# Moving taps and transposes off VectorE, pairing its exponential chains, and doubling convolution streams in an attention-and-convolution kernel

## The chip, the cores and the metric

The kernel runs on one core of one Trainium2 chip. A core has TensorE (PE), VectorE (DVE), ScalarE (ACT), GpSimd (POOL) and SyncE (SP), the last used here to issue transfers. The metric is device time in microseconds (us), the median of the runs of one program. Bytes are moved by 16 DMA engines.

## What is computed

Two independent halves are computed and concatenated along the last axis. S = 2048 positions, D = 640 channels, bf16.

```python
# half A: a gated long convolution
k_shift[s] = sum_t k[s - t] * shift_k[:, t]        # 4 taps, per channel
kv = k_shift * v
y  = causal_convolution(kv, ssm_k)                 # per channel, length 2048 (by FFT in the reference)
a  = q * (y + kv * ssm_D)
# half B: attention with H = 32 heads of 20 channels
q, k, v = split(x @ wqkv)
p = softmax(q @ k.T / sqrt(20));  b = (p @ v) @ wo
out = concatenate([a, b], -1)                      # (1, 2048, 1280)
```

## The kernel before

**Attention.** The scores are computed transposed, in blocks of 128 keys x 512 queries. There are 4 query chunks, 8 groups of 4 heads and 16 key blocks, so 512 steps of 4 heads: 2048 such blocks, numbered as units (`NU`). A unit is one matmul with 20 rows of the array (`S_task`, L594); up to three units go into neighbouring PSUM banks, in two alternating halves of three banks. One ScalarE instruction takes the exponential of two or three banks at once and writes bf16 into slots of `P_sb` (`EXP_task`, L635, L640). `NPU` = 24 slots exist. `PV_task` (L681) multiplies four slots with V, which carries a column of ones for the softmax sum, and frees them. At the end of a group VectorE copies the sums out (L700), TensorE transposes them and VectorE divides (L706 to L721); the output projection follows (L766).

**Exponentials on VectorE.** Part of the units goes to VectorE instead, in a chain of seven instructions per unit (`chain_start`, L651): L664 reads PSUM, scales and adds so that the uint16 result is nearly the bit pattern of the bf16 exponential; L666 takes the low seven bits; L667, L668, L670 and L671 form a polynomial correction; L672 adds it. All but L664 read and write SBUF only. `want_vec` (L1134) decides, for each third bank, whether it goes to VectorE: only if the planned queue of VectorE is below `VQ` = 3 us, and not for the last two key blocks of a group.

**The order of work is written by a planner.** The Python code keeps an estimated clock per engine (`Prog.op`, L141) with a cost for every instruction, and while it emits the program it picks what TensorE and VectorE do next by what would be ready and by due times. Projections (`KQ_task`, L490; `V_task`, L498), transposes of x (`XT_task`, L434) and output tasks are put in a list with due times, counted in steps of four units (L1046 and the lines after). Matmuls on zeros (`zeros`, L346, L349) are put in when the planned TensorE stream of the last 3.4 us is under `ZTH` = 1.8 us. What the hardware executes is this fixed order per engine, with semaphore waits.

**Half A, taps.** x and k arrive with positions on partitions. For x, TensorE transposes 128x128 tiles into PSUM (L420) and VectorE or ScalarE copies them to `xT` (L432, L430). For k, `kv_iter` (L528) gets four shifted copies of k from memory per tile of 128 positions and does the four taps and the product with v on VectorE: eight operations of 128x640 per tile (L531), 16 tiles. The product goes to scratch in memory, once in order (`kv_scratch`) and once with reversed blocks of 32 (`kvr_scratch`).

**Half A, convolution.** When the taps are done, `conv_setup` (L866) starts it. A channel's convolution is a product with a Toeplitz matrix, whose tiles are read from the padded kernels in memory with a step of one element between partitions: `hk_load` (L887) loads 4 x [32, 2112] per quarter task, into one of four buffers. Per quarter task 32 matmuls run (L929), with 128 rows of weights each and 16 x shrinking numbers of columns, 5120 in all. The moving operand is built by 80 GpSimd copies (`kvx_build`, L893, L899) into a buffer whose other channels are zero. VectorE adds the halves out of PSUM (L947, L948, L950). `A_iter` (L963, L969) then does the product with D, the sum and the product with q on VectorE, three operations of 128x320 for each of 32 pieces.

Of the kernel before, what the change touches and what calls it, by code (L numbers as in the profile page):

```python
# [6 lines left out]
ALU = mybir.AluOpType  # L7
FP32 = mybir.dt.float32
BF16 = mybir.dt.bfloat16
I32, I16, U16 = mybir.dt.int32, mybir.dt.int16, mybir.dt.uint16  # L10

S = 2048
# [11 lines left out]
HKW = 2112  # L24
NHK = 4
NPU = 24
NQS = 10
NU = NB * 4
NPAIR = 48
NXB = 3  # L30
KV0, KVPACE, APACE, VQ, CONVE, ZTH, AGE, WAIT3 = 30.0, 0.75, 0.5, 3.0, 60, 1.8, 14, 0.3
TAND = 0.287
# [3 lines left out]
EXP_C = (0.07826797, 0.30457564)  # L36
LAT = {"pe": 0.12, "act": 0.1, "dve": 0.06, "pool": 0.1}
# [42 lines left out]
class Prog:  # L80
    ENGS = ("sp", "act", "pe", "dve", "pool")

    def __init__(self, nc, enter):
# [11 lines left out]
        self.stream = []  # L95
        self.sem = {e: self.newsem("s_" + e) for e in self.ENGS if e != "sp"}
# [44 lines left out]
    def op(self, eng, fn, reads=(), writes=(), tok=True, dsem=None, extra=(), n=1, c=0.1, kb=0.0, st=0.0, kind="f", two=False, me=None):  # L141
# [42 lines left out]
        if dsem is not None:  # L184
            self.dma_t = max(self.dma_t, start + 1.7) + kb / 215
            when = self.dma_t + 0.5
# [33 lines left out]
    def dmas(self, eng, pairs, dsem, reads=(), writes=()):  # L220
# [3 lines left out]
        def fn(e):  # L224
            for i, (out, in_) in enumerate(pairs):
                ins = e.dma_start(out, in_)
                if i + 1 < len(pairs):
                    ins.then_inc(s, 16)
            return ins
        kb = 0.0  # L230
        for out, _ in pairs:
# [3 lines left out]
            kb += e  # L235
        return self.op(eng, fn, reads, writes, dsem=dsem, n=len(pairs), c=0.43 * len(pairs), kb=kb)
# [10 lines left out]
def build_kernel(nc, A_q, A_k, A_v, A_shift_k, A_ssm_k, A_ssm_D, B_x, B_wqkv, B_wo, out):  # L247
# [3 lines left out]
    with ExitStack() as es:  # L251
# [15 lines left out]
        P_sb = sb("P_sb", [128, NPU, 512])  # L267
# [4 lines left out]
        XV_sb = sb("XV", [128, NXB, 512], U16)  # L272
        XF_sb = sb("XF", [128, NXB, 3, 512])
# [3 lines left out]
        Dbc = sb("Dbc", [128, D])  # L277
        ident = sb("ident", [128, 128])
        ZS = sb("ZS", [128, 256], FP32)
        rden = sb("rden", [128, 32], FP32)  # L280

        HK_E, KVR_E, KVX_E, Y_E, AST_E = HKW, 64 * 80, 8 * 256, 16 * 320, 320
        ph0 = NCC * 2 * D + 4 * 4 * D + 2 * 5 * D + KS * D + 2 * D + 2 * D
        ph1 = NHK * HK_E + KVR_E + 2 * KVX_E + 2 * Y_E + 5 * AST_E
        xT = sb("xT", [128, NCC, S])
        WQ = sb("WQ", [128, NCC, D])
        R = sb("R", [128, max(ph0, ph1)])
# [8 lines left out]
        xst = [carve(4 * D).rearrange("p (t d) -> p t d", t=4) for _ in range(4)]  # L296
        kst = [carve(5 * D).rearrange("p (j d) -> p j d", j=5) for _ in range(2)]
        Ctile = carve(KS * D).rearrange("p (j d) -> p j d", j=KS)
        tA, tB = carve(D), carve(D)
        kvst = [carve(D) for _ in range(2)]  # L300
        pos[0] = 0
        HK = [carve(HK_E) for _ in range(NHK)]
        KVr = carve(KVR_E).rearrange("p (j c) -> p j c", j=64)
        KVX = [carve(KVX_E) for _ in range(2)]
        Y = [carve(Y_E).rearrange("p (t c) -> p t c", t=16) for _ in range(2)]
        Aq = [carve(AST_E) for _ in range(3)]
        Akv = [carve(AST_E) for _ in range(2)]
# [8 lines left out]
        kvd = nc.dram_tensor("kv_scratch", (S, D), BF16).ap()  # L316
        kvr_d = nc.dram_tensor("kvr_scratch", (S, D), BF16).ap()

        b_ident, b_ones, b_tA, b_tB, b_C, b_ZS = (Buf() for _ in range(6))
        b_WK0, b_WQ0, b_Wa, b_Wb, b_Wo, b_D = (Buf() for _ in range(6))  # L320
        b_xst = [Buf() for _ in range(4)]
# [3 lines left out]
        b_XV, b_XF, b_XQ, b_XP = ([Buf() for _ in range(NXB)] for _ in range(4))  # L325
# [8 lines left out]
        b_kst = [Buf(), Buf()]  # L334
        b_kvst = [Buf(), Buf()]
        b_kvd, b_kext, b_kshT = [], Buf(), Buf()
# [27 lines left out]
        def x_load(n):  # L364
            return P.dma("sp", xst[n], ap(x2, [[D, 128], [128 * D, 4], [1, D]], n * 512 * D), DS("x%d" % n),
                         writes=[b_xst[n]])

        b_x0 = [Buf() for _ in range(4)]
        for i in range(4):
            P.dma("sp", xst[0][:, i, :], x2[i * 128:(i + 1) * 128, :], DS("x0%d" % i), writes=[b_x0[i]])  # L370
# [1011 lines left out]
```

## Time and profile before

The median of three runs is 880.22 us (878.06 to 895.95). The profiled execution has a span of 882.1 us and took 883.89 us.

| what | from the profile of before |
|---|---|
| span | 882.1 us |
| units on ScalarE / on VectorE | 1845 / 203 |
| matmuls of the convolution (L929) | 5120 |
| GpSimd copies (L899) | 80, 1368 ns each |
| matmuls on zeros (L349) | 178 |
| loads of convolution weights | 640, 132 KB each |
| mean DMA rate | 146 GB/s |

In the profile a group line has the form "line, engine, operation, written tile <- read tile, shape, count | busy us, mean ns of one | idle time before it, and the releaser of most of it". The rows of digits cut the span into 40 slices of 22 us; a digit is the busy share in tenths, in the row PEclk the TensorE clock that was granted. A table by stage has, after the stage and its length, the busy us of each engine with the number of instructions in brackets, then the granted clock, the share of DMA time and GB/s. Neighbouring instructions of an engine overlap a little, so the sum of groups is larger than the engine's busy time.

### The profile page before, as it was taken

To read this page: it belongs to the slowest core of one execution; us is meant where nothing else is said; L and a number is where in the kernel's file an instruction comes from. 1 tells how busy PE (TensorE), PEld (TensorE's weight loads), DVE (VectorE), ACT (ScalarE), POOL (GpSimd) and SP (SyncE) were. 2 spreads that over 40 slices of the span, in tenths; PEclk is the share of its full clock that TensorE was granted. 3 is DMA by queue.
4 is the path that set the end of the run, shared out by engine and by line. 5 is a ranking of instruction groups with operands and counts; after the bars stand their busy time and mean duration, and the time that the engine had idled before them with its cause. 6 is when DMAs were issued, how large, how long until landed. Compare 5 with 4: busy or idle time off the path is not lost.

```text
span 882.1 us, 26786 instructions
## 1 busy us (share of the span) xinstructions
PE 831.9 (94%) x11389; PEld 389.3 (44%) x11402; DVE 770.3 (87%) x1993; ACT 843.9 (96%) x731; POOL 121.0 (14%) x94
## 2 busy tenths in 40 slices
PE   9999999988999999999999999899999999989887
PEld 5432332222345545545545545444454554545422
DVE  4469999999479998999899999999899999989963
ACT  6699999999779999999999999999999999999996
POOL 3000000001402220122210220220120122010000
PEclk9999999999569999999999999999999999999999
DMA  9614333334736556565669656767454465645243
GB/s 298 208 58 153 105 106 106 106 106 75 149 90 174 162 155 174 165 163 149 184 172 172 169 150 180 192 174 193 133 148 127 136 178 139 174 125 159 56 109 86
DMA packets 83603, 129.19 MB, mean 146 GB/s; under 512 B 34561, under 2 KB 60283, under 8 KB 83483
## 3 DMA queue, kind: packets, MB, share of 16 engines
q1 hardware_dynamic: 81323, 124.36, 52.5%
q0 software_dynamic: 704, 2.74, 0.8%
q8 instruction: 90, 1.47, 0.7%
q10 hardware_dynamic: 1456, 0.37, 0.2%
q14 instruction: 30, 0.25, 0.1%
HBM read 116.81 MB, written 13.23 MB: 147 GB/s over the span
## 4 chain that ended last, share of the span: by engine, by line
DVE 48%; PE 27%; ACT 22%; issue 2%; DMA 1%; DVEq 0%; SPq 0%
ACT P_sb L640 22%; DVE XV L664 9%; PE PS L929 8%; PE PS L598 8%; DVE XF L671 6%; DVE P_sb L672 6%; DVE XF L670 5%; PE PS L690 5%; DVE R L531 3%; DVE XF L667 3%; DVE XF L666 3%; DVE XF L668 3%; PE PS L446 2%; PE PS L349 2%; DVE R L950 2%
## 5 line engine op out<-in xcount | busy, mean ns | idle before, releaser
L640 ACT ACTIVATE P_sb<-PS 128x1536 bf16<-128x1536 f32 (+1 forms) x723 | 839.4, 1356 | 24.6 <-PE PS L598 23.6
L598 PE MATMUL PS<-QT,KT 20*128 20x512 bf16 x2048 | 286.3, 392 | 25.6 <-ACT P_sb L640 17.1
L929 PE MATMUL PS<-R 128*128 128x128 bf16 (+15 forms) x5120 | 250.3, 195 | 2.4 <-DVE Bout L764 1.0
L929 PEld LDWEIGHTS PS<-R 128*128 128x128 bf16 x5120 | 200.8, 98 | 113.2 <-issue 112.8
L690 PE MATMUL PS<-P_sb,V_sb 128*21 128x512 bf16 x2048 | 179.1, 391 | 9.5 <-DVE P_sb L672 8.4
L899 POOL COPY R<-R 32x512 bf16<-32x512 bf16 x80 | 109.4, 1368 | 449.4 <-PE PS L929 438.6
L664 DVE TENSOR_SCALAR XV<-PS 128x512 uint16<-128x512 f32 x203 | 139.2, 686 | 32.2 <-PE PS L598 31.4
L598 PEld LDWEIGHTS PS<-QT,KT 20*128 20x128 bf16 x2048 | 70.4, 91 | 181.3 <-ACT P_sb L640 130.5
L672 DVE TENSOR_TENSOR P_sb<-XF,XV 128x512 uint16<-128x512 bf16 x203 | 90.3, 445 | 4.8
L671 DVE TENSOR_TENSOR XF<-XF 128x512 bf16<-128x512 bf16 x203 | 90.2, 444 | 3.6
L670 DVE TENSOR_TENSOR XF<-XF 128x512 bf16<-128x512 bf16 x203 | 87.7, 432 | 0.0
L690 PEld LDWEIGHTS PS<-P_sb,V_sb 128*21 128x21 bf16 x2048 | 38.6, 89 | 91.0 <-issue 46.7
L667 DVE TENSOR_SCALAR XF<-XF 128x512 bf16<-128x512 uint16 x203 | 64.7, 319 | 1.9
L531 DVE TENSOR_TENSOR R<-R 128x640 bf16<-128x640 bf16 x128 | 61.6, 487 | 3.6 <-DMA R<-in_A_v_dram 0.7
L668 DVE TENSOR_SCALAR XF<-XF 128x512 bf16<-128x512 uint16 x203 | 63.0, 310 | 0.0
L349 PE MATMUL PS<-Zt 128*128 128x512 bf16 x178 | 58.3, 421 | 1.3 <-DVE Zt L343 1.0
L666 DVE TENSOR_SCALAR XF<-XV 128x512 uint16<-128x512 uint16 x203 | 57.2, 301 | 0.2
L446 PE MATMUL PS<-xT,WQ 128*20 128x512 bf16 (+1 forms) x660 | 46.4, 374 | 1.8 <-DVE R L950 0.8
L446 PE MATMUL PS<-xT,R 128*20 128x512 bf16 (+2 forms) x660 | 45.2, 374 | 0.4 <-DVE QT L432 0.2
L504 PE MATMUL PS<-R,xT 128*128 128x160 bf16 (+1 forms) x240 | 31.3, 257 | 1.0 <-ACT P_sb L640 0.8
L432 DVE CAST KT<-PS 128x512 bf16<-128x512 f32 (+1 forms) x32 | 21.6, 674 | 11.2 <-PE PS L446 11.1
L876 POOL MEMSET R<- 128x2048 bf16 x2 | 3.7, 1826 | 188.4 <-PE PS L690 188.4
(54 smaller groups left out, 339.7 us busy)
## 6 DMA issues: line engine op xcount, KB each, us to landing
R<-kext_scratch SPq DMA_DIRECT2D x640, 132.0 KB, 2.9
R<-in_A_k_dram SPq DMA_DIRECT2D x15, 640.0 KB, 3.9
kext_scratch<-in_A_ssm_k_dram POOLq DMA_DIRECT2D x1, 2560.0 KB, 14.3
R<-in_A_v_dram SPq DMA_DIRECT2D x16, 160.0 KB, 5.4
kv_scratch<-R SPq DMA_DIRECT2D x16, 160.0 KB
kvr_scratch<-R SPq DMA_DIRECT2D x16, 160.0 KB
R<-kvr_scratch SPq DMA_DIRECT2D x8, 320.0 KB, 7.0
R<-in_A_q_dram SPq DMA_DIRECT2D x32, 80.0 KB, 2.1
```

The lines of the kernel that those rows point to most:

```text
L446: ins = e.matmul(bank[bk][32 * i:32 * i + DH, 0:n], Wt[:, cc, off + i * DH:off + (i + 1) * DH], xT[:, cc, x0:x0 + n], start=(cc == 0), sto ...
L598: ins = e.matmul(bank[b0 + i], KT[32 * u:32 * u + DH, g, kb * 128:(kb + 1) * 128], QT[32 * u:32 * u + DH, qs(qc, g), :], start=True, stop= ...
L640: P.op("act", lambda e: e.activation(P_sb[:, s0:s0 + m, :], PS[:, b0 * 512:(b0 + m) * 512].rearrange("p (u q) -> p u q", u=m), ACT.Exp, sc ...
L664: (lambda e: e.tensor_scalar(V, bank[bk], scale * 1.4426950408889634 * 128.0, 127.0 * 128.0, op0=ALU.mult, op1=ALU.add), [bkb[bk]], [bv], ...
L667: (lambda e: e.tensor_scalar(Q, F.bitcast(U16), -128.0, None, op0=ALU.add), [bf], [bq], 0.287, True),
L668: (lambda e: e.tensor_scalar(C, F.bitcast(U16), a / 16384.0, b / 128.0, op0=ALU.mult, op1=ALU.add), [bf], [bc], 0.287, True),
L670: (lambda e: e.tensor_tensor(Q, Q, F.bitcast(U16), ALU.mult), [bf, bq], [bq], 0.421, True),
L671: (lambda e: e.tensor_tensor(Q, Q, C, ALU.mult), [bq, bc], [bq], 0.421, True),
L672: (lambda e: e.tensor_tensor(P_sb[:, z, :].bitcast(U16), Q, V, ALU.add), [bv, bq], [b_P[z]], 0.421, True)], end)
L690: ins = e.matmul(bank[OBANK][32 * u:32 * u + DH + 1, :], V_sb[:, kb, 4 * g + u, :], P_sb[:, slot[4 * b + u], :], start=first, stop=last, t ...
L899: P.op("pool", lambda e, dst=dst, src=src: e.tensor_copy(dst, src), reads=[cv["KVr"]], writes=[cv["KVX"][i]] if X == 3 else [], extra=(cv[ ...
L929: P.op("pe", lambda e, o=o, lhsT=lhsT, rhs=rhs, st=st, last=last: e.matmul(o, lhsT, rhs, start=st, stop=last, skip_group_check=True), read ...
```

## The change

Five things change together, with a retuned planner.

- x and k are loaded by transposing transfers directly into the layout with channels on partitions. The transposes on TensorE and their evacuations go away.
- The four taps become matmuls on TensorE: the transposed k, shifted by one column per tap, against diagonal matrices `Dg` that GpSimd builds once (20 tasks of 16 matmuls, `C_task`). VectorE multiplies the sum in PSUM by v while it takes it out. The D term is folded into the first element of each convolution kernel, so that `kv_scratch` and two of the three final operations disappear; the third, the product with q, goes to GpSimd in 128 pieces of 128x160.
- Two exponential chains on VectorE run as one: each unit has its own PSUM read, and the other operations take both units, 128x1024, six instructions for two. `want_vec` is allowed a planned queue of 5 us and opens no pair in the last three key blocks of a group.
- The convolution is retiled: 16 channels per task, weights as 4 x [32, 4, 544] per quarter task; each matmul streams its operand and, beside it, an equal number of zeros into other columns, 52 to 64 columns in all.
- GpSimd's copies and products are each put beside a VectorE instruction that reads PSUM (`pool_beside`). Loads and stores on SyncE are issued in the order in which the planner expects them to be ready.

P slots grow from 24 to 36, four of which become free only when the taps' buffers are dead. The filler goal is 2.1 us in 3.4.

The core of the diff:

```diff
-NPU = 24
+NPU, NPX = 36, 4
+OBS = 20
-KV0, KVPACE, APACE, VQ, CONVE, ZTH, AGE, WAIT3 = 30.0, 0.75, 0.5, 3.0, 60, 1.8, 14, 0.3
+KBV, KBW, LONE = 13, 12, 16
+CQ = 0.026
+KV0, KVS, VQ, CONVE, ZTH, AGE, WAIT3 = 52, 2.5, 5, 80, 2.1, 40, 0.2
...
+        if turn:
+            def fn(e):
+                return e.dma_start_transpose(*pairs[0])
...
+        def x_load(t, n):
+            return P.dmas("sp", [(xT[:, :, t * 128:(t + n) * 128], x2[t * 128:(t + n) * 128, :])], DS("x%d" % t),
+                          writes=b_xT[t:t + n], slow=1.3, turn=True)
...
-        def kv_iter():
...
+        def C_task(c, h, bk):
...
+                    for j in range(KS):
+                        ins = e.matmul(bank[bk][:, n * 128:(n + 1) * 128], kT[i][:, cc, 16 + 128 * t - j:144 + 128 * t - j],
+                                       Dg[:, j, cc, :], start=(n + j == 0), stop=(j == KS - 1), skip_group_check=True)
...
+            work(1, [(lambda e: e.tensor_tensor(o, p, v, ALU.mult), [bkb[bk], b_vst[i]], [b_kvst[i]], 0.69, False)], after)
...
+            V, F, Q = XV_sb[:, i, 0:512 * m], XF_sb[:, f, 0, 0:512 * m], XF_sb[:, f, 1, 0:512 * m]
+            one, two = 0.154 + 0.1335 * m, 0.154 + 0.267 * m
...
+                (lambda e: e.tensor_scalar(F.bitcast(U16), V, 127, None, op0=ALU.bitwise_and), bv, [bf], one, True),
+                (lambda e: e.tensor_scalar(Q, F.bitcast(U16), -128.0, None, op0=ALU.add), [bf], [bq], one, True),
+                (lambda e: e.tensor_tensor(Q, Q, F.bitcast(U16), ALU.mult), [bf, bq], [bq], two, True),
+                (lambda e: e.tensor_scalar(F, F.bitcast(U16), a / 16384.0, b / 128.0, op0=ALU.mult, op1=ALU.add), [bf], [bf],
+                 one, True),
+                (lambda e: e.tensor_tensor(Q, Q, F, ALU.mult), [bf, bq], [bq], two, True)] + last, end)
...
+            P.dmas("sp", [(HK[qd % NHK][32 * a:32 * a + 32].rearrange("p (c x) -> p c x", c=4),
+                           ap(kext, [[1, 32], [KXL, 4], [1, HKW]], 4 * qd * KXL + KPAD - 63 + 512 * a)) for a in range(4)],
...
+                        rhs = sub(KVX[i], [[(2 - i) * KVX_E - p, 1 if st else 2], [64, 2], [2, n]], p)
+                        o = sub(bank[MISC], [[-16 if u + x else 16, 1 if st else 2], [256, 2], [1, n]], (4 * u + x) * 16 + d)
...
+        def pool_beside(t, start, end):
+
+            for w in pworks[:4]:
+                fn, rd, wr, c, _ = st = w.steps[0]
+                if P.T["pool"] > start + 0.1 or P.ready("pool", rd, wr, st) > start + 0.1 or start + c > end + 0.02:
+                    continue
+                P.op("pool", fn, reads=rd, writes=wr, c=c, me=st, extra=[t])
```

## The prediction

> **What bounds the kernel now.** I read the page's busy shares and slices first, then the groups, the waits, and a table by stage.
>
> ```profile
> PE 831.9 (94%) x11389; PEld 389.3 (44%) x11402; DVE 770.3 (87%) x1993; ACT 843.9 (96%) x731; POOL 121.0 (14%) x94
> ACT  6699999999779999999999999999999999999996
> PEclk9999999999569999999999999999999999999999
> ```
>
> ScalarE is busy 96% of the span, and the span is nearly its sum: first exponential at 10.1 us, 839.4 us of exponentials, 24 us of gaps, 8.8 us of tail. PE's 94% is modelled from pipelined matmuls. So the time moves only by (a) exponential blocks taken from ScalarE, (b) its gaps, (c) the two ends.
>
> ```profile
> L640 ACT ACTIVATE P_sb<-PS 128x1536 bf16<-128x1536 f32 (+1 forms) x723 | 839.4, 1356 | 24.6 <-PE PS L598 23.6
> L664 DVE TENSOR_SCALAR XV<-PS 128x512 uint16<-128x512 f32 x203 | 139.2, 686 | 32.2 <-PE PS L598 31.4
> L672 DVE TENSOR_TENSOR P_sb<-XF,XV 128x512 uint16<-128x512 bf16 x203 | 90.3, 445 | 4.8
> L667 DVE TENSOR_SCALAR XF<-XF 128x512 bf16<-128x512 uint16 x203 | 64.7, 319 | 1.9
> L531 DVE TENSOR_TENSOR R<-R 128x640 bf16<-128x640 bf16 x128 | 61.6, 487 | 3.6 <-DMA R<-in_A_v_dram 0.7
> ```
>
> Of 2048 blocks of 128x512, VectorE computes 203 by its seven-operation chain and ScalarE 1845. VectorE's capacity therefore sets the split. Stages (us, PE, PEld, DVE, ACT, POOL busy, clock, DMA share, GB/s):
>
> ```profile
> 0.00:44.00 44.00, 41.73 (x533) 21.87 (x533) 20.22 (x51) 29.53 (x34) 7.87 (x12) 1.00 0.78 254
> 66.00:220.00 154.00, 142.03 (x1553) 42.58 (x1553) 148.04 (x357) 152.78 (x130) 3.65 (x2) 0.99 0.36 108
> 220.00:260.00 40.00, 39.97 (x324) 15.16 (x323) 21.70 (x53) 29.80 (x24) 10.88 (x8) 0.53 0.55 120
> 300.00:800.00 500.00, 477.16 (x7352) 251.93 (x7359) 468.00 (x1235) 495.76 (x433) 89.20 (x66) 1.00 0.62 161
> ```
>
> ScalarE loses 10.2 us in 220-260 us, where TensorE's clock is halved, and 1.2 us just before. One 7.0 us gap lies at 22.2-29.3 us: twelve exponentials of two blocks have filled all 24 P buffers, while PE runs projections and x transposes; the first P·V matmuls (28.1 us) free them. All other gaps sum to about 5 us. In 300-800 us VectorE is 93.6% busy with 145 chains, 29 per 100 us.
>
> [...] beside the 3.71 us GpSimd memset pair at 213.8 us one L667 takes 1.04 us. [...]
>
> **Part by part.**
>
> *VectorE work removed.* k's taps (L531, 128 x 487 ns), the tap copies (4 x 490), the final A products (L969, 96, 32 us) and the x evacuations (L432, 17, 7 us). Summed group times exceed VectorE's 770 us by 100 us over 1993 instructions, so each overlaps its neighbour by 0.05 us: I subtract that. 55 + 2 + 27 + 6 = 90 us leave. Twenty tap evacuations from PSUM come, priced like L664: 20 x 0.64 = 13 us. Non-chain work: 770 − 203 x 2.59 (below) = 245 before, 245 − 90 + 13 = 168 after.
>
> *Paired chains.* Now 0.686+0.301+0.319+0.310+0.432+0.444+0.445 = 2.94, less 7 x 0.05, is 2.59 us a block. A pair keeps two PSUM reads (1.37) and runs six double operations: three one-source each +0.133 (1.33), three two-source each +0.267 (2.12). 4.82 − 8 x 0.05 = 4.42, or 2.21 us a block. Bounds: 2.59 (nothing saved) and 2.05 (GpSimd delays gone as well). I take 2.18, as the measured means contain GpSimd delays that the placement beside PSUM reads should partly remove.
>
> *New waits.* The first block of a pair has no result until its partner's S exists (at most 16 blocks, `LONE`). Only its P·V waits; the order is written by readiness, so other P·V go ahead on TensorE, and eight or twelve more buffers hold the results. The PSUM bank is released by the read, which stays single. A GpSimd operation waits for the VectorE instruction before its slot; behind it stand only GpSimd's own. Tap evacuations wait for v, loaded tens of us earlier. I price these at 1 us of the end in all.
>
> *How many blocks move.* Until 40 us VectorE does some 14 us (20 less 6); until 24 us before the end I let it be 94.5% busy (93.6% now; the longer allowance of queued work helps); then 8 us. With T = 840: 14 + 0.945 x 776 + 8 = 755; less 168, over 2.18: n = 269. That is 66 more than 203. A block costs ScalarE 0.42 us: in the trace triples end 1.305 us apart, (11.99 − 1.55)/8, pairs 0.885 us, (3.77 − 1.11)/3. The instruction count stays: a triple becomes two plus one. Gain 66 x 0.42 = **28 us**.
>
> *Gaps.* P buffers go from 24 to 32 (36 later), x transposes leave PE (80 instructions) and the P·V bank stops serving projections after 20 blocks (`OBS`): of 7 us I credit **5**. Filler zeros now aim at more activity (2.1 instead of 1.8 us per window): of 11.4 us I credit **10**.
>
> *The start.* x tiles come transposed. Today the first tile is used at 3.5 us and the last is evacuated at 7.4; K starts at 6.9. Bounds: as fast as plain loads, 2 us gained; 30% slower and queued, 2 us lost. I take **0**.
>
> *TensorE.* Taps add 320 matmuls of 128 columns: 20 x 0.9 = 18 us, within 66-220 us. The zeros there already show slack at the end of that stage (22 in 176-220 us), so the last K projections slip, not the exponentials. The convolution keeps 5120 matmuls; one now streams 52-64 columns, half of them zeros. Twenty in a row of 80 columns and fewer take 0.70 us: (0.70 − 0.18)/19 = 27 ns. 5120 x 27 = 138 us. Before, 16-256 columns at 2400 per us with that floor give about 179. Net minus 23 us with x transposes gone; PE is not the end of the chain, so this only shields S.
>
> *GpSimd.* 80 copies of 1.37 us become 80 smaller ones (the code assumes 0.56), plus 128 products (0.42): 99 us against 109 now. Bounds of harm: 0, or each of 208 blocking VectorE for half its length, 50 us = 23 blocks = 10 us of the end.
>
> *DMA.* A quarter's weights come as 512 packets of 1088 B instead of 128 of 4224 B. In 88-176 us packets of 2.03 KB on average cost 101 ns, 20 GB/s an engine, so 54 ns per 1088 B; upper bound the mean packet of 300-800 us, 111 ns (43,673 in 60.6% of 8000 engine-us). I take 70: 81,920 x 70/16 = 358 us. Smaller pieces: 41,000 of 160 B at 18 ns (8192 landed within 9 us after 215.5 us), 33,000 of 320 B at twice that: 46 + 74 = 120 us. 478 us in a stage of some 590: hidden, as four quarters are loaded ahead. SyncE issues behind each other: a quarter's four issues take 4 x 0.42 us now; with the code's 0.475 it is 1.9 us of every 3.7.
>
> Sum: 880.2 − 28 − 5 − 10 = **837 us**; 1 us for the new waits: **838**.
>
> **Rivals.**
> *Clock halves again* (chance 0.12). The changed kernel has less real PE work, and S, P·V and filler must carry the gap before the convolution. For: it happened under the same plan's care. Against: doubled streams and more filler. Two stretches of 10 us: 858.
> *GpSimd eats the gain* (0.10). For: instructions of VectorE run up to 1365 ns instead of 287 beside GpSimd. Against: most windows are one-PSUM-input reads. n = 240: 838 + 12, and 2 for later P·V: 852.
> *More blocks* (0.04). VectorE 97% busy at 2.05 us: 14 + 0.97 x 762 + 8 − 168 = 593, n = 289: 20 x 0.42 = 8, start gains 2: 828.
> *Weights arrive late, slower than before* (0.06). Packets at 111 ns: 568 + 120 = 688 us from about 214 us, where it starts now (the last K projections, due at block 120, still precede it): the convolution ends at 902, and with evacuation, products and stores 10 later: 912. For: DMA share already 0.62. Against: in 88-176 us small packets ran at full rate per byte.
>
> **How the numbers follow.** Forecast 0.68, rivals 0.12, 0.10, 0.04, 0.06. The range 820 to 860 takes the bounds of the pair cost (2.05 gives n = 286 and 831; 2.59 gives 227 and 856), of the start and of three rivals; some 0.15 stays outside. Faster by over 2% means under 862.6: all of the forecast, of the fast rival and nearly all of the first two: 0.88. Within 2%: 0.06. Slower: 0.06, the DMA rival.
>
> **What would show it.** Chain reads from PSUM (as L664) about 269; double operations near 0.44 and 0.71 us; ScalarE about 812 us; no 5 in the clock row; the gap before 30 us under 3 us; DMA share near 0.75 in the convolution. A first exponential after 13 us, VectorE operations over 1 us in number, or TensorE waiting for convolution weights would prove steps wrong.

## The result, and the profile after

The changed kernel takes 856.51 us in the median (856.18 to 857.93) against 882.51 us (878.06 to 895.95) for the kernel before on the same chip: a ratio of 0.9725, 95% interval 0.9676 to 0.9774. It is faster, by 26 us where the forecast had 42. The profiled execution has a span of 853.9 us (before: 882.1). Ratios, here and below, leave out executions that were disturbed, so a ratio can differ from the quotient of two medians.

The busy shares and two rows of slices of the changed kernel:

```profile
PE 819.9 (96%) x11683; PEld 380.6 (45%) x11694; DVE 775.2 (91%) x1560; ACT 811.3 (95%) x748; POOL 96.4 (11%) x160
ACT  5878799999999999999999999999999999999996
PEclk9989999999999999999999999999999999999999
```

The 5 in the clock row and the two sevens beside it in ScalarE's row are gone. In their place stand a 7, an 8 and a 7 in ScalarE's slices 3 to 5, at 43 to 107 us. VectorE is busy 775.2 us, 5 us more than before, in 433 fewer instructions.

The groups of the changed kernel that answer to those of before (L661 is the exponential on ScalarE, L681 to L721 belong to the chain on VectorE, L948 is GpSimd's copy):

```profile
L661 ACT ACTIVATE R<-PS 128x1024 bf16<-128x1024 f32 (+1 forms) x742 | 807.8, 1230 | 26.8 <-PE PS L619 25.2
L681 DVE TENSOR_SCALAR XV<-PS 128x512 uint16<-128x512 f32 x289 | 197.5, 685 | 16.3 <-PE PS L619 13.3
L721 DVE TENSOR_TENSOR XF<-XF 128x1024 bf16<-128x1024 bf16 x145 | 103.6, 716 | 0.3
L718 DVE TENSOR_TENSOR XF<-XF 128x1024 bf16<-128x1024 bf16 x145 | 98.4, 683 | 0.2
L719 DVE TENSOR_SCALAR XF<-XF 128x1024 bf16<-128x1024 uint16 x145 | 60.5, 419 | 0.4
L948 POOL COPY R<-R 128x256 uint32<-128x256 uint32 x80 | 51.1, 638 | 377.6 <-DVE XF L721 114.1
```

VectorE reads 289 blocks from PSUM (203 before), the double operations take 0.42 and 0.68 to 0.72 us, and ScalarE is busy 807.8 us instead of 839.4. But ScalarE's idle time is 26.8 us, more than the 24.6 us of before. The span is again almost a sum: first exponential at 10.7 us, 807.8, 26.8, and 8.6 us after.

Where that idle time lies is read from the table by stage (busy us of PE, PEld, DVE, ACT, POOL, then clock, DMA share, GB/s):

```profile
0.00:44.00 44.00, 40.11 (x484) 17.46 (x488) 12.81 (x31) 30.60 (x33) 5.16 (x11) 0.96 1.01 236
44.00:66.00 22.00, 17.45 (x179) 6.76 (x171) 19.55 (x35) 16.52 (x18) 5.55 (x3) 0.84 0.16 47
66.00:100.00 34.00, 33.51 (x433) 12.71 (x432) 30.90 (x61) 26.40 (x26) 0.00 (x0) 1.00 0.01 1
220.00:260.00 40.00, 39.26 (x586) 18.05 (x584) 37.36 (x74) 40.00 (x39) 3.84 (x6) 1.00 0.59 124
300.00:800.00 500.00, 485.86 (x7713) 246.91 (x7716) 483.97 (x993) 493.97 (x446) 66.80 (x116) 1.00 0.85 179
```

The same table for two stages of the kernel before:

```profile
44.00:66.00 22.00, 20.97 (x271) 7.85 (x263) 14.72 (x32) 22.00 (x18) 0.00 (x0) 1.00 0.18 57
66.00:100.00 34.00, 31.74 (x357) 10.18 (x357) 31.69 (x75) 34.00 (x30) 0.00 (x0) 1.00 0.41 134
```

In 220 to 260 us ScalarE is now busy all 40 us (29.8 before): the clock's part came in the size expected. In 44 to 100 us it was never idle before and now loses 5.5 and 7.6 us. These 13.1 us are most of what the forecast lacks.

The first part of them, in the timeline of the changed kernel (start, length, instruction, idle time before it and what ended it):

```profile
53.60 5.35 DVE L721 TENSOR_TENSOR XF<-XF 128x1024 bf16<-128x1024 bf16 x1
53.78 4.62 POOL L592 TENSOR_TENSOR R<-ident,SK 128x2560 bf16<-128x2560 bf16 x1
59.58 1.46 PE L739 MATMUL PS<-R,V_sb 128*21 128x512 bf16 x12 [4.33 <-DVE R L713]
61.63 1.02 ACT L661 ACTIVATE R<-PS 128x1024 bf16<-128x1024 f32 x1 [5.00 <-PE PS L619]
```

GpSimd builds the diagonals `Dg` (L592) in one instruction of 4.62 us. VectorE's L721, 0.68 us elsewhere in the median, started 0.18 us before it and lasts until GpSimd is done. The paired result (L713) comes late, P·V waits 4.33 us for it, and ScalarE 5.00 us for the next S. TensorE's clock is lower in this stage too (0.84); without the stall it is 1.00 (experiment 5). The kernel before has such stalls too, on a smaller scale. Of the six chain operations that read and write SBUF only, 72 overlap a GpSimd instruction there, and the longest of each line takes 1.27 to 1.44 us; none of the other 1146 takes over 0.43 us. L664, which reads PSUM, takes 0.67 to 0.70 us in all 203 cases, 22 of them beside GpSimd. So in these traces GpSimd at times holds up VectorE's work on SBUF, and never L664's reads of PSUM; by what means, and which of the two goes first, they don't show. Here the VectorE operation, first by 0.18 us in the profile, was the one that waited.

### The profile page after: what moved, and what is told of

The parts are those of the page before. It is cut to its first block, busy times and chain, and to the rows that moved or that the text cites. A ratio compares the mean times of both kernels' runs of the same rounds, so it can differ in the third digit from the quotient of the medians.

```text
span 853.9 us, 27281 instructions
## 1 busy us (share of the span) xinstructions
PE 819.9 (96%) x11683; PEld 380.6 (45%) x11694; DVE 775.2 (91%) x1560; ACT 811.3 (95%) x748; POOL 96.4 (11%) x160
## 4 chain that ended last, share of the span: by engine, by line
PE 50%; ACT 33%; DVE 15%; issue 1%; DMA 0%; SPq 0%; DVEq 0%
ACT R L661 33%; PE PS L974 17%; PE PS L619 15%; PE PS L739 8%; PE PS L473 5%; DVE XV L681 3%; DVE XF L721 2%; PE PS L381 2%; PE PS L825 2%; PE PS L522 1%; DVE R L711 1%; DVE ZS L991 1%; DVE ZS L990 1%; DVE R L993 1%; DVE XF L718 1%
## 5 line engine op out<-in xcount | busy, mean ns | idle before, releaser
L661 ACT ACTIVATE R<-PS 128x1024 bf16<-128x1024 f32 (+1 forms) x742 | 807.8, 1230 | 26.8 <-PE PS L619 25.2
L974 PE MATMUL PS<-R 128*128 128x60 bf16 (+4 forms) x5120 | 212.1, 195 | 0.2 <-DVE R L993 0.2
L681 DVE TENSOR_SCALAR XV<-PS 128x512 uint16<-128x512 f32 x289 | 197.5, 685 | 16.3 <-PE PS L619 13.3
L974 PEld LDWEIGHTS PS<-R 128*128 128x128 bf16 x5120 | 176.0, 98 | 79.0 <-issue 77.7
L739 PE MATMUL PS<-R,V_sb 128*21 128x512 bf16 x2048 | 168.2, 385 | 9.3 <-DVE R L713 5.6
L721 DVE TENSOR_TENSOR XF<-XF 128x1024 bf16<-128x1024 bf16 x145 | 103.6, 716 | 0.3
L718 DVE TENSOR_TENSOR XF<-XF 128x1024 bf16<-128x1024 bf16 x145 | 98.4, 683 | 0.2
L948 POOL COPY R<-R 128x256 uint32<-128x256 uint32 x80 | 51.1, 638 | 377.6 <-DVE XF L721 114.1
L711 DVE TENSOR_TENSOR R<-XF,XV 128x1024 uint16<-128x1024 bf16 x92 | 63.0, 686 | 0.2
L719 DVE TENSOR_SCALAR XF<-XF 128x1024 bf16<-128x1024 uint16 x145 | 60.5, 419 | 0.4
L717 DVE TENSOR_SCALAR XF<-XF 128x1024 bf16<-128x1024 uint16 x145 | 59.9, 420 | 0.1
L716 DVE TENSOR_SCALAR XF<-XV 128x1024 uint16<-128x1024 uint16 x145 | 59.7, 419 | 0.2
L713 DVE TENSOR_TENSOR R<-XF,XV 128x512 uint16<-128x512 bf16 x105 | 40.5, 419 | 0.1
```

The costliest lines, as they stand in the source:

```text
L661: P.op("act", lambda e: e.activation(P_sb[:, s0:s0 + m, :], PS[:, b0 * 512:(b0 + m) * 512].rearrange("p (u q) -> p u q", u=m), ACT.Exp, sc ...
L681: work(0.2, [(lambda e: e.tensor_scalar(V, bank[bk], scale * 1.4426950408889634 * 128.0, 127.0 * 128.0, op0=ALU.mult, op1=ALU.add), [bkb[b ...
L711: last = [(lambda e: e.tensor_tensor(o, Q2, V2, ALU.add), bv + [bq], [b_P[z] for z in zs], two, True)]
L717: (lambda e: e.tensor_scalar(Q, F.bitcast(U16), -128.0, None, op0=ALU.add), [bf], [bq], one, True),
L718: (lambda e: e.tensor_tensor(Q, Q, F.bitcast(U16), ALU.mult), [bf, bq], [bq], two, True),
L719: (lambda e: e.tensor_scalar(F, F.bitcast(U16), a / 16384.0, b / 128.0, op0=ALU.mult, op1=ALU.add), [bf], [bf], one, True),
```

## The experiments

The kernel before took 879.5 to 882.7 us in the median on the chips used; each ratio is to it on the same chip. "Changed kernel" below is the one above, at 0.9725.

**1. Chains one by one.** The changed kernel, but each pair is closed as soon as it has one block.

```diff
             opened.append(z)
-            if h:
-                chain_end()
+            chain_end()
```

> The changed kernel with one edit: each chain is closed after one unit, so VectorE runs its six further operations on 128x512 again. Everything else of the change stays. Theory P (pairing buys blocks): a block costs VectorE 2.18 us in pairs in the changed kernel (1.37 + 1.26 + 1.40 + 0.73 us of measured means a pair, less 8 x 0.05, halved) and about 2.55 alone; with the same busy time 289 blocks become some 247, 42 x 0.42 us = 18 us go back to ScalarE, less up to 7 us because results hold P slots for less time: 867 to 875 us. Theory F (what was freed on VectorE does it all, pairing only delays P·V): 850 to 858 us, block count within 10 of 289.

Measured: 868.05 us (866.87 to 869.39), ratio 0.9865 (0.9834 to 0.9897).

```profile
L681 DVE TENSOR_SCALAR XV<-PS 128x512 uint16<-128x512 f32 x250 | 170.8, 685 | 34.9 <-PE PS L619 32.3
L720 DVE TENSOR_TENSOR XF<-XF 128x512 bf16<-128x512 bf16 x250 | 108.5, 436 | 0.9
```

Theory P held. With the other edits alone VectorE does 250 blocks, 47 more than before; pairing adds 39 and is worth some 12 us (868.05 − 856.51 = 11.5; 12.3 by the ratios, of 880).

**2. Only the pairs.** The kernel before with the changed kernel's paired chains and its `want_vec`, two buffers for pairs and the 24 P slots that it had.

```diff
-XV_sb = sb("XV", [128, NXB, 512], U16)
+XV_sb = sb("XV", [128, NXB, 1024], U16)
...
-NXB = 3
+NXB = 2
+KBV, KBW, LONE = 13, 12, 16
```

> The kernel before with the paired chains alone (functions of the changed kernel, its queue limit of 5 us and its age limit; two buffers for pairs instead of three, for lack of memory). The 24 P slots, the taps on VectorE and everything else stay as before. Theory P without slots: 0.4 us saved a block on 203 blocks is 82 us of VectorE, 31 more blocks, 13 us: about 868 us. Theory S (pairs keep results away for longer, so they need the slots): ScalarE's gaps for want of P slots grow by as much as the blocks save or more: 878 to 895 us, with more blocks on VectorE than 203 and ScalarE gaps well over 25 us.

Measured: 888.43 us (885.62 to 907.07), ratio 1.0080 (1.0051 to 1.0110). The profiled execution has a span of 898.6 us, so of its groups the counts and ScalarE's busy time are read, and of the gaps only that they are many:

```profile
L642 ACT ACTIVATE P_sb<-PS 128x1536 bf16<-128x1536 f32 (+1 forms) x737 | 831.1, 1279 | 48.6 <-PE PS L600 46.8
L662 DVE TENSOR_SCALAR XV<-PS 128x512 uint16<-128x512 f32 x234 | 159.2, 685 | 44.2 <-PE PS L600 41.9
```

VectorE takes 31 blocks more than before and ScalarE is busy 8 us less, yet the kernel is slower by its ratio. In the kernel before, with its 24 slots and with two buffers for pairs instead of three, pairs cost more than they move. That this is for want of slots is argued, with experiment 3; the missing third buffer was not tested apart.

**3. Fewer slots.** The changed kernel with 28 P slots for 36.

```diff
-NPU, NPX = 36, 4
+NPU, NPX = 28, 4
```

> The changed kernel with 28 P slots instead of 36 (24 instead of 32 until the taps are done). Theory S (slots carry the pairs): ScalarE waits for slots many times; gaps grow from 27 us to 50 or more: 875 to 895 us. Rival (slots only matter at the start and at 80 to 92 us): 2 us more at the start, nothing after: 857 to 861 us.

Measured: 894.84 us (889.32 to 899.35), ratio 1.0149 (1.0095 to 1.0202). Its groups, and then its table by stage:

```profile
L661 ACT ACTIVATE R<-PS 128x1024 bf16<-128x1024 f32 (+1 forms) x751 | 806.7, 1191 | 71.7 <-PE PS L619 68.8
```

```profile
100.00:220.00 120.00, 115.06 (x1335) 44.45 (x1331) 113.93 (x220) 96.76 (x99) 3.50 (x2) 0.99 0.30 65
```

ScalarE's busy time is that of the changed kernel (806.7), its idle time 45 us larger; in 100 to 220 us it idles 23 us, where the changed kernel idles 1. (The profiled execution took 899 us; two of the four took 889 and 890.) Without the eight slots the whole gain of the change is gone.

**4. No more blocks than before.** The changed kernel, but `want_vec` lets only 203 blocks go to VectorE, spread evenly.

```diff
-            if not 60 < k < NU - 34 or not opened and not xfree:
+            if nvec[0] > 203 * (k - 60) / (NU - 94) or not 60 < k < NU - 34 or not opened and not xfree:
```

> The changed kernel, but no more blocks go to VectorE than before: at most 203, spread evenly. It splits the change into blocks moved and all the rest. Theory B (blocks are the gain): 86 x 0.42 = 36 us go back to ScalarE, less the stalls for slots (7 us) that then go: 882 to 888 us, so no gain over the kernel before. Theory R (rest of the change, such as TensorE relieved and the undisturbed clock, gives 10 us or more of its own): 866 to 874 us.

Measured: 885.47 us (883.72 to 888.80), ratio 1.0063 (1.0042 to 1.0083).

```profile
PE 838.6 (95%) x11804; PEld 383.0 (43%) x11804; DVE 643.1 (73%) x1241; ACT 845.1 (96%) x733; POOL 96.6 (11%) x160
L661 ACT ACTIVATE R<-PS 128x1536 bf16<-128x1536 f32 (+1 forms) x727 | 841.6, 1320 | 21.9 <-PE PS L619 19.8
```

Here VectorE is idle 27% of the time and nothing is gained. Taken together, transposing loads, taps on TensorE and retiled convolution bring no time of their own: ScalarE regains the 10 us of 220 to 260 us here too (clock 1.00, 39.6 us busy), but it loses 3.1 us in 44 to 66 us, 4.7 in 100 to 220 and 6.6 in 300 to 800, where before it lost 0, 1.2 and 4.2. What they bring is room on VectorE, and the blocks moved into it are the gain: 29 us for 86 blocks.

**5. Dg built early.** Order unchanged; SK, the tap coefficients, comes over ScalarE's queue and GpSimd builds `Dg` at 5.9 us.

```diff
+        P.dma("act", SK, ap(A_shift_k, [[KS, 128], [128 * KS, NCC], [1, KS]]), DS("sk"), writes=[b_SK])
+        P.op("pool", lambda e: e.tensor_tensor(
+                Dg, ...
...
-            P.dma("sp", SK, ap(A_shift_k, [[KS, 128], [128 * KS, NCC], [1, KS]]), d_sk, writes=[b_SK])
...
-            P.op("pool", lambda e: e.tensor_tensor(
-                Dg, ...
```

> The changed kernel with the same order of instructions on TensorE, ScalarE and VectorE; only GpSimd's product that builds the diagonal tap matrices is moved to its first microseconds, with the taps loaded by ScalarE's queue at the start. Lock theory: the VectorE operation of 5.35 us beside it at 53.6 us becomes 0.68, the ScalarE gap of 5.0 us at 56.6 us and the half clock of 50 to 70 us go: 848 to 852 us. Rival (that time was borrowed from the stalls at 80 to 92 us, which wait for P slots anyway): 855 to 857 us, with longer gaps there.

Measured: 849.70 us (848.60 to 851.68), ratio 0.9661 (0.9635 to 0.9687). Its table by stage:

```profile
44.00:66.00 22.00, 21.18 (x247) 8.19 (x243) 21.58 (x49) 22.00 (x24) 1.03 (x2) 1.00 0.18 46
66.00:100.00 34.00, 33.44 (x417) 13.60 (x415) 30.88 (x62) 26.62 (x26) 0.00 (x0) 1.00 0.14 29
```

ScalarE is busy all 22 us of the stage in which it lost 5.5, and TensorE's clock is full. One GpSimd instruction at the wrong moment cost some 6 us (856.51 − 849.70 = 6.8; 5.6 by the ratios, whose intervals just overlap, so the stage shows the cause better than the ratios show the size). The 7.4 us of 66 to 100 us stay.

**6. What made Dg late, first try.** GpSimd had waited 24.5 us for HD, two small loads (the kernels' first elements and D) of which SyncE issued the first only at 47.8 us. GpSimd adds them before it builds `Dg`. SyncE's issue of the transposing k loads had lasted 6.5 and 12.5 us. So the first two k loads were made plain, with the same bytes and destination; in those two quarters k is not transposed.

```diff
-            P.dmas("sp", [(kT[i][:, :, z:528], k2[c * 512 - 16 + z:c * 512 + 512, :])], d_kT[i], writes=[b_kT[i]], slow=1.3, turn=True)
+            n = 528 - z
+            src = ap(k2, [[5 * n, 128], [n, 5], [1, n]], (c * 512 - 16 + z) * D) if c < 2 else k2[c * 512 - 16 + z:c * 512 + 512, :]
+            P.dmas("sp", [(kT[i][:, :, z:528], src)], d_kT[i], writes=[b_kT[i]], slow=1.3, turn=c > 1)
```

> The changed kernel with the first two of the four loads of k plain (same bytes, same destination, in 1 KB pieces) instead of transposing; k is not transposed in these two quarters, so what is computed from them isn't the reference's. Order unchanged. Theory Q (the transposing loads held SyncE's queue for 6.5 and 12.5 us, so HD came late, so the GpSimd instruction that builds Dg ran beside VectorE's tile operations at 54 to 58 us): HD's loads are issued before 35 us, Dg is built before 46 us, the 5.0 us gap of ScalarE at 56 to 61 us is gone and the time is 847 to 853, as in the run with Dg built early. Rival R (HD's loads wait for buffers or for data, not for the queue): HD still at 48 us or later and 854 to 858.

Measured: 857.94 us (856.81 to 859.65), ratio 0.9762 (0.9708 to 0.9816): no gain. The waits of SyncE's queue in this run, and GpSimd's timeline:

```profile
SPq L588 <- DMA Wo_sb<-in_B_wo_dram: 16.3, 1, 16.3
```

```profile
49.90 4.63 POOL L594 TENSOR_TENSOR R<-ident,SK 128x2560 bf16<-128x2560 bf16 x1
```

SyncE was through with its other loads at 28.2 us, and then waited 16.3 us for Wo to land. HD shares Wo's semaphore, and the program lets a load on a semaphore wait for the one before it. HD came at 44.5 instead of 47.8 us. The transposing loads account for some 3 us of HD's delay and are not the cause.

**7. What made Dg late, second try.** The changed kernel with HD's two loads on semaphores of their own, order unchanged.

```diff
-                 writes=[b_D], dsem=d_small, c=0.475)
-            P.dma("sp", HD[:, 1, :], ap(A_ssm_D, [[5, 128], [1, 5]]), d_small, writes=[b_D])
+                 writes=[b_D], dsem=DS("hd0"), c=0.475)
+            b_D1 = Buf()
+            P.dma("sp", HD[:, 1, :], ap(A_ssm_D, [[5, 128], [1, 5]]), DS("hd1"), writes=[b_D1])
```

> The changed kernel with the two small loads of HD on semaphores of their own, where the changed kernel makes the first wait for the load of Wo, with which it shares one, and the second for the first; order unchanged. Theory W (that wait, 6.1 us and 1.8 us in the trace of the changed kernel, is what made the Dg instruction late, since loading k plainly left HD at 44.5 us with a wait of 16.3 us on Wo): HD issued at 41.7 and 42.2 us, Dg built between 45 and 51 us, the 5.35 us operation of VectorE gone or below 2.5 us, 849 to 854. Rival R (the DMA engines are full until 47 us, so HD lands as late as before): HD sum after 50 us and 855 to 858.

Measured: 859.74 us (857.87 to 861.38), ratio 0.9740 (0.9723 to 0.9757): no gain either. SyncE's, GpSimd's and VectorE's timeline in this run:

```profile
43.20 0.69 SPq L586 DMA_DIRECT2D HD<-in_A_ssm_k_dram  x1
43.94 0.98 SPq L234 DMA_DIRECT2D HD<-in_A_ssm_D_dram  x1
51.09 0.22 POOL L592 TENSOR_TENSOR HD<-HD 128x5 bf16<-128x5 bf16 x1 [21.46 <-DMA HD<-in_A_ssm_D_dram]
52.34 4.63 POOL L595 TENSOR_TENSOR R<-ident,SK 128x2560 bf16<-128x2560 bf16 x1
52.55 4.71 DVE L722 TENSOR_SCALAR XF<-XF 128x1024 bf16<-128x1024 uint16 x1
```

The wait is gone and HD is issued at 43.2 and 43.9 us, but GpSimd has it only at 51 us: some 7 us after the issue, where the second of the changed kernel's lands in 2.2 us. It was issued directly behind Wo's 800 KB. The DMA engines were busy for most of that time: their share is 1.12 in 11 to 44 us and 0.23 in 44 to 66, that is 5 us of full work, which reach to 49 us if they lie together. So rival R held, HD is late because of the bytes that go ahead of it; waiting at the issue or behind other transfers makes little difference. Among these bytes are also the 2.5 MB of `ssm_k` that GpSimd's queue copies to `kext_scratch` from 28.9 us on. This time it is a one-source operation of VectorE that stands still, for 4.71 us. Which transfers would have to move was not tried; experiment 5 goes round the question, as `Dg` needs no HD.

**8. GpSimd at any time.** GpSimd's copies and products lose their wait for the VectorE instruction beside which they were put.

```diff
-                P.op("pool", fn, reads=rd, writes=wr, c=c, me=st, extra=[t])
+                P.op("pool", fn, reads=rd, writes=wr, c=c, me=st)
```

> The changed kernel without the wait that holds each GpSimd copy and product until a VectorE instruction that precedes a PSUM read is done; they start as soon as their inputs and GpSimd's queue allow. Placement theory: each of some 144 operations of 0.45 to 0.6 us then starts beside any VectorE operation, and about two in three of VectorE's are of the kind that blocks: 144 x 2/3 x about 0.3 us = 29 us of VectorE, 13 blocks, 5 to 8 us: 861 to 865 us, with slower means of the double operations. Rival (queueing on GpSimd spreads them anyway): 855 to 858 us.

Measured: 881.03 us (874.11 to 898.89), ratio 1.0006 (0.9982 to 1.0031). Two groups, and a stage of its table:

```profile
L716 DVE TENSOR_SCALAR XF<-XV 128x1024 uint16<-128x1024 uint16 x145 | 69.6, 489 | 0.1
L948 POOL COPY R<-R 128x256 uint32<-128x256 uint32 x80 | 67.0, 837 | 373.0 <-PE PS L974 291.7
```

```profile
700.00:760.00 60.00, 57.18 (x694) 27.37 (x694) 49.44 (x95) 47.43 (x43) 11.48 (x18) 0.74 0.76 167
```

The expectation had the direction; the loss is three to five times the 5 to 8 us that it gave. GpSimd's copy grows from 638 to 837 ns and L716 from 419 to 489 (446 without its longest, of 5.41 us), while L681, which reads PSUM, stays at 684 (685). "Two in three" was a little high: 922 of the changed kernel's 1560 VectorE instructions are chain operations on SBUF alone. VectorE's busy time rises by 21 us. Beyond that, ScalarE's idle time rises from 26.8 to 51.0 us, with the clock at 0.74 for 60 us on end. The kernel without the wait is some 24 us slower (881.03 − 856.51 = 24.5; 24.7 by the ratios), nearly all of the change's gain. But its order is not the same throughout: up to 440 us VectorE and ScalarE run the changed kernel's instructions and are 4.2 us late, 0.4 of it from the start; after that the planner, which no longer sees the wait, wrote another order. How much of the 24 us is the missing wait and how much the other order isn't told apart.

**9. Streams without zeros.** Each convolution matmul streams only its operand; order unchanged.

```diff
-                        rhs = sub(KVX[i], [[(2 - i) * KVX_E - p, 1 if st else 2], [64, 2], [2, n]], p)
-                        o = sub(bank[MISC], [[-16 if u + x else 16, 1 if st else 2], [256, 2], [1, n]], (4 * u + x) * 16 + d)
+                        rhs = sub(KVX[i], [[64, 2], [2, n]], p)
+                        o = sub(bank[MISC], [[256, 2], [1, n]], (4 * u + x) * 16 + d)
```

> The changed kernel in the same order, but each convolution matmul streams its 26 to 32 real columns alone, without the zeros beside them (5120 matmuls; the results are the same). Clock theory (the zeros keep TensorE's clock up): there is idle time between the matmuls, the clock falls in the convolution and ScalarE waits: 875 us or more, with digits under 9 in the clock row between 240 and 780 us. Rival (the other matmuls keep it up; a matmul of 32 columns takes the same 25 to 27 ns as one of 64): 853 to 858 us, clock at full.

Measured: 899.49 us (880.61 to 936.59), ratio 1.0097 (1.0050 to 1.0145). The table by stage is of an execution with a span of 895.4 us:

```profile
220.00:260.00 40.00, 38.61 (x570) 16.41 (x567) 37.58 (x74) 40.00 (x40) 3.84 (x6) 1.00 0.57 121
300.00:800.00 500.00, 487.25 (x7271) 214.12 (x7263) 457.22 (x939) 468.21 (x423) 68.22 (x114) 0.87 0.80 170
```

TensorE has less to stream and is slower: its clock is 0.87 on average in 300 to 800 us where it was 1.00. In 220 to 260 us it is full without the zeros, too. The rival's figure for a matmul is near what the kernel before shows: there a convolution matmul of 32 columns is followed by the next after 25 ns in the median, one of 64 columns after 29. The zeros beside the operand are worth some 33 us by the ratios (1.0097 − 0.9725, of 880) and 43 us by the medians (899.49 − 856.51).

**10. One tap of four.** Of each C tile's four diagonal products only one is made (three taps of the shift convolution are left out); order unchanged.

```diff
-                    for j in range(KS):
+                    for j in range(1):
...
-                                       Dg[:, j, cc, :], start=(n + j == 0), stop=(j == KS - 1), skip_group_check=True)
+                                       Dg[:, j, cc, :], start=(n + j == 0), stop=True, skip_group_check=True)
```

> The changed kernel with one of the four diagonal products of each C tile (3 x 80 of 320 matmuls gone, each some 55 ns, so about 13 us less TensorE work); the order and everything else are as they were. Three of the four taps of the shift convolution are left out. Theory H (the taps on TensorE lie in its free time, ScalarE and VectorE set the end): within 2.5 us of the changed kernel, 854 to 859. Rival T (TensorE, 96% busy, is part of the path while the taps run): 843 to 850, with shorter gaps of ScalarE between 60 and 240 us.

Measured: 866.84 us (866.28 to 872.79), ratio 0.9872 (0.9819 to 0.9925): neither theory, some 10 us slower. Its table by stage, of an execution with a span of 870.6 us (the three others had 864 to 865):

```profile
170.00:180.00 10.00, 10.00 (x70) 1.70 (x66) 7.50 (x14) 7.48 (x8) 0.00 (x0) 0.50 0.11 34
180.00:190.00 10.00, 10.00 (x79) 2.32 (x76) 6.51 (x12) 7.30 (x7) 0.00 (x0) 0.55 0.11 33
```

240 matmuls fewer, and the clock halves, here and again in 200 to 220 us (0.50).

**11. Three taps on zeros.** All 320 matmuls are back, but for three taps the diagonals are zeros, so that these taps are again left out.

```diff
-                                       Dg[:, j, cc, :], start
+                                       Zt[:, 0:128] if j else Dg[:, j, cc, :], start
```

> The changed kernel with the diagonals of three of the four taps replaced by zeros: all 320 matmuls of the C tiles run, three quarters of them on zeros (three taps of the shift convolution are left out, as in one_tap_same). Theory D (with one tap alone the clock fell to 0.50 between 170 and 220 us because TensorE had less to do there; what the matmuls multiply doesn't matter): 853 to 860, the clock at 1.00 from 100 to 300 us. Rival E (the fall came with something else in that run, such as values or the moment at which other work arrived): 862 to 872 and a clock below 0.9 somewhere in 150 to 230 us.

Measured: 860.12 us (857.58 to 867.03), ratio 0.9773 (0.9728 to 0.9818). The same stage as above:

```profile
170.00:180.00 10.00, 9.99 (x123) 3.50 (x121) 9.90 (x20) 10.00 (x11) 0.00 (x0) 1.00 0.12 34
```

The clock is full again, as theory D had it, though the median lies 0.1 us above its range. What TensorE multiplied didn't matter to the clock here, only that it worked: with less to do the clock was 0.87 in 300 to 800 us (experiment 9) and 0.50 in 170 to 180 us (experiment 10), with work on zeros in the same places 1.00.

**12. A version with other constants.** `Dg` early, 37 slots, and other constants of the planner, so another order.

```diff
-NPU, NPX = 36, 4
+NPU, NPX = 37, 4
...
-KBV, KBW, LONE = 13, 12, 16
+KBV, KBW, LONE = 14, 13, 8
...
-KV0, KVS, VQ, CONVE, ZTH, AGE, WAIT3 = 52, 2.5, 5, 80, 2.1, 40, 0.2
+KV0, KVS, VQ, CONVE, ZTH, AGE, WAIT3 = 68, 2.75, 4.5, 80, 2.1, 34, 0.15
```

> The changed kernel with Dg built at 6 us (SK loaded by ScalarE's queue), 37 P slots for 36, and other constants for the planner (KBV 14, KBW 13, LONE 8, KV0 68, KVS 2.75, VQ 4.5, AGE 34, WAIT3 0.15, OBS 24), so another order: 19 blocks more or fewer on VectorE are possible. Theory: Dg early gives 5 to 7 us as before, one slot and the order 2 to 5 us more by fewer gaps of ScalarE between 60 and 100 us: 843 to 849. Rival (the gaps there come from VectorE's work, not from slots and order): 849 to 853.

Measured: 853.10 us (849.11 to 858.35), ratio 0.9705 (0.9654 to 0.9756): above what the theory gave. Its table by stage:

```profile
66.00:100.00 34.00, 32.72 (x386) 9.55 (x378) 33.74 (x67) 34.00 (x33) 0.00 (x0) 1.00 0.01 2
460.00:480.00 20.00, 19.59 (x223) 10.71 (x213) 13.43 (x27) 14.06 (x14) 1.64 (x3) 0.59 0.67 152
```

The loss in 66 to 100 us is gone, so it wasn't forced by VectorE's work. But in this execution, of 858 us, the clock fell to 0.59 at 460 to 480 us, which costs ScalarE 5.9 us, and 6.4 us go in 220 to 260 us. The two fastest of the six, at 849 us, had a mean clock of 0.996 where this one had 0.986. Of the versions run, the one of experiment 5 has the lowest median; this one isn't told apart from it with certainty.

## Why the prediction was right, and where it missed

Forecast and measurement, term by term, in the span of the profile:

| term | forecast | measured |
|---|---|---|
| blocks on VectorE | 269 | 289 |
| ScalarE busy with exponentials | 839.4 − 28 = 811.4 | 807.8 |
| ScalarE's gaps | 24.6 − 15 + 1 = 10.6 | 26.8 |
| first exponential | 10.1 | 10.7 |

The gaps are 16 us longer than forecast and ScalarE's work 4 us shorter; that is the difference in the span. The result lies within the forecast's range, but near its end, and not by the steps that set that end: 860 came from the pair's upper cost (856 us) and the clock rival (858 us), and neither happened. The gap that did happen was in no bound, so that the range held is in part luck.

**Bound and direction: right.** ScalarE still sets the span, and blocks moved to VectorE are the gain. Experiment 4 shows it: without the blocks the ratio is 1.006.

**VectorE's work and the pair cost: right, a little low in effect.** The chain operations sum to 683 us. Over 1560 instructions the overlap is 0.06 us each (group sums of 868 us against 775 busy), so the 1211 chain operations take 610 us, 2.11 us a block; with the forecast's 0.05 it is 2.15. The forecast had 2.18. What a second block adds, +0.133 and +0.267 us, was an estimate that equals the planner's constants in the diff and that no trace had shown; in the changed kernel L717 takes 0.280 us for one block (a single case) and 0.421 for two, L718 0.413 and 0.685, so 0.14 and 0.27. (The last operation is double in 92 pairs only; in the others it is two single ones.) Work outside the chains is 165 us (forecast 168), VectorE is busy 775 us (forecast 755). (775 − 165)/2.11 = 289. Of the 20 blocks too few, some 9 come from the price of a block, 6 from a span 14 us longer than the 840 us of the sum, and 5 from the share at which VectorE ran between 40 and 830 us, 95.8% and not 94.5%. The rival "More blocks" counted 289 as well, at 97% and 2.05 us a block, but expected 828 us from them.

**A block's worth: 0.37 us for 0.42.** 839.4 − 807.8 = 31.6 us for 86 blocks. ScalarE makes 742 exponentials instead of 723, which the forecast held constant. More blocks at less each: the two misses pull in opposite directions, and 31.6 us stand for the forecast's 28.

**The gaps: wrong, and this is the step that failed.** "Of 7 us I credit 5": in 11 to 44 us ScalarE idles 5.1 us where it idled 7.8, so 2.7 came back. "Of 11.4 us I credit 10": right in the number, ScalarE is full in 220 to 260 us. But "New waits … I price these at 1 us" measured 13.1 us in 44 to 100 us, where ScalarE had never been idle:
- 5.5 us come from the one instruction that building `Dg` added (experiment 5). The forecast counted GpSimd's copies and products and bounded their harm, but not this setup operation of 4.6 us: it is longer than six of VectorE's operations and was queued behind a late load.
- 7.6 us come with pairs at their full number: singly closed chains lose 0.4 us there, and 203 blocks in pairs 0.8. In the timeline of the changed kernel both gaps of this stage, 3.07 and 4.37 us, end alike: a pair's last operation ends (83.38 and 90.93 us), then P·V starts (83.55, 90.99), then S for ScalarE (83.88, 91.53). This fits results that come late; but TensorE works on projections and taps meanwhile, so its order may be the cause as well. That the number of slots matters is shown by experiment 3, that another order can avoid the loss by experiment 12; which of both makes this very gap isn't told apart.

**GpSimd: the low end of its bounds held for the placed operations.** Leaving out the 5.35 us case, L721's mean is (103.6 − 5.35)/144 = 0.68 us, that of an undisturbed double operation (0.68 in the 123 cases that overlap no GpSimd instruction). The placement rests on PSUM reads standing clear of GpSimd, and they do: L681 takes at most 0.69 us in all 289 cases, 84 of them beside GpSimd. In the run without the placement all of the gain is gone (experiment 8). The rival "GpSimd eats the gain" named a real danger; its 14 us lie between the 4 us lost while the order is still the same and the 24 us in all. The products are 64 pieces of 128x160, not the 128 that the list of changes and the forecast counted.

**Taps on TensorE: hidden, as forecast, and more than that.** Their time doesn't show in the span; taking three quarters of them away made it 10 us longer (experiment 10). They do the filler's work: in 100 to 220 us the changed kernel runs 6 matmuls on zeros where the kernel before ran 32. The net of TensorE's groups is near the forecast too: convolution 212.1 us for 250.3, taps 25.1, transposes of x 6.6 gone, together minus 20 (forecast minus 23); both convolution sums are some 70 us above the forecast's 138 and 179. Of its two rates one is in the trace: two matmuls on zeros of 512 columns take 0.61 us (at 206.99 us of the kernel before) and four 1.04, so 0.215 us each, 2380 columns per us. The other, 27 ns a matmul, is low: 34 in a row take 1.23 us (at 411.36 us of the changed kernel), 32 ns each after the first.

**Clock: right in the number, not by the reasons given.** The rival "clock halves again" stayed away. The credit of 10 us was for a higher filler goal, but in 220 to 260 us the changed kernel runs 6 matmuls on zeros where the kernel before ran 18; the added ones lie behind 300 us. Nor are the doubled streams the reason there: without them the clock is 1.00 in this stage as well (experiment 9). They hold it up later, in the convolution. With the old goal and pairs alone it is 1.00 in this stage, too (experiment 2). In the kernel before the clock fell after a stretch with less TensorE work: 8.48 us busy in 205 to 215 us, 0.91 in 215 to 217, and from 217 us a clock of 0.50; in the changed kernel TensorE is busy 9.73 us in the first and 1.90 in the second of these stretches. What filled them, and how little work it takes for the clock to fall, isn't told apart, so what kept it up there stays open, and these 10 us are in part luck. Nor does the kernel before always lose them: on the chip of experiments 4, 8 and 9 its fastest execution took 874.16 us at a mean clock of 0.996, where the profiled one had 0.977.

**DMA: right that it is hidden, and nearly right in size.** From 218 us to the end the hardware queue's 155,048 packets took 76.9% of 16 engines' time, 489 us or 50 ns each, against 478 us for weights and smaller pieces; the share in 300 to 800 us is 0.85, not 0.75. Per byte they were slower: 102.7 MB at 76.9% are 13 GB/s an engine for packets of 662 B on average, where the kernel before had 20 in 88 to 176 us at 2.03 KB, as in its first 44 us (254 GB/s at a share of 0.78). TensorE waits 0.2 us in all before L974, so weights are never late.

## What to carry to other kernels

Moving work to an engine with room gains only where its results come back in time: before pricing such a change, count the buffers that hold the delayed results, and look at each long one-off instruction that comes to lie beside the engine's work (4.62 us of GpSimd cost some 6 us here). An instruction added to set something up belongs in the profile's first microseconds, not behind the last load of the start (849.70 us for 856.51). And removed TensorE work can cost more than it took: 240 matmuls fewer made the kernel 10 us slower here, with the clock at 0.50 to 0.55 for 40 us. Ask what keeps the array busy afterwards.

## What the hardware showed that was not expected

- A GpSimd operation of 4.6 us held up a VectorE operation that, by the profile, started 0.2 us before it (5.35 us for 0.68), and in another run a one-source one that started 0.2 us after it (4.71 us for 0.42).
- 240 matmuls of TensorE fewer made the kernel 10 us slower, with the clock at 0.50 to 0.55 in two stretches of 20 us; matmuls on zeros in their place brought it back.
- Issuing a transposing load of some 512 rows of k held SyncE's queue for 6.5 and 12.5 us, where a plain load of the same bytes took 1.7 and 1.8 us. That brought no time here (experiment 6).
